# The last slice of a spectral convolution in halves, and its first output tile in two column parts

## The chip, the cores and the metric

The kernel runs on one core of one Trainium2 chip. The metric is device time in microseconds (us) of one execution. The core has five engines with instruction queues of their own: TensorE (PE in the profile, with PEld for its weight loads), VectorE (DVE), ScalarE (ACT), GpSimd (POOL) and SyncE (SP, which here only issues DMAs). Each engine takes its own instructions in order, and waits for others through semaphores.

## The reference

Four stages follow each other on a sequence x of 2048 tokens with 512 channels, each adding its result to x:

```
x = x + A(layernorm(x))     # long convolution, one filter per channel
x = x + B(layernorm(x))     # local dilated attention
x = x + A(layernorm(x))
x = x + B(layernorm(x))
```

A makes a filter K of 2048 lags for every channel from the state space parameters, multiplies the transforms of filter and input, transforms back, and adds u * Dskip:

```
y = irfft(rfft(u padded to 4096) * rfft(K padded to 4096))[:2048] + u * Dskip
```

B projects to q, k and v (32 heads of 16), lets every token attend to 8 tokens at distances 0, 2, ..., 14, and projects back. All data are bfloat16.

## The kernel before

The filters' spectra are computed once, at the start, and lie in DRAM (`kt_scratch`). Both A stages use them. `a_steps` builds one convolution. The transform has two stages: the first leaves Z, and then the 512 channels are taken in 16 slices of 32 channels, numbered cg from 0 to 15. A slice goes through a relay of steps, each named by a letter:

- T (L250): eight transposes of Z on TensorE into PSUM, `pt`; t (L256): the copy `zt` of it to SBUF, on VectorE mostly.
- X (L262): two matmuls of 512 columns, `xp`; c (L266): ScalarE copies them to `xc`, 128 x 1024, bfloat16.
- p (L270): VectorE multiplies `xc` with the spectrum `Kt` of the slice, which a DMA has brought (L232), into `pab`, 128 x 2048.
- v (L281): the inverse second stage, 16 pairs of a weight load (from `pab`) and a matmul of 128 columns, into `vp`, two PSUM banks for eight groups g.
- V (L285): ScalarE copies `vp`, reordered, to the slice's 32 of the 512 channels of VT.

In the first convolution the order of these steps stands at the end of the string KGEN, written out by hand (L336 to L354; it ends `@v13 @c15 @v14 @V13 @p15 @V14 @v15 @V15`). In the second it is the loop of `a_layer` (L299 to L310). `vp` and the tiles that follow share two PSUM buffers (tag psg in the first, psS in the second), so v of slice 15 needs the buffer that V of slice 13 frees, and the first y tile the one that V of slice 14 frees.

Then the inverse first stage: `y_rows(g, hf)` (L317) fills a PSUM tile `ps_y` of two times 128 rows x 512 channels, with three matmuls of 512 columns each: two against VT (L323, L324) and one with the identity that adds the old X (L327). The last group, g = 3, has a fourth (L326), which adds a correction `kU` for the last token. `kU` is computed by four VectorE instructions on one partition (L314 and three at L316), which are issued after the last instruction that `a.last` names: the product p of slice 15.

`b_layer` takes the eight tiles one by one. `y_group` (L1345) makes ScalarE copy each to X (L1361; with row sums at L1356 for two rows of group 1 in the first B stage), and `norm` follows for each group of four rows: statistics on VectorE (L1057, aggregated at L1060), logarithm and exponential on ScalarE (L1063, L1064), the bias (L1065) and the normalised rows N (L1073 on VectorE, L1071 on ScalarE). TensorE transposes N (L1087), ScalarE and VectorE copy it to `xnT` (L1090), and the q and k projections begin (L1104). The order of B's instructions comes from a planner (`Plan`) with estimated durations; the framework that builds the program then places instructions of neighbouring parts among each other.

Of the kernel before, what the change touches and what calls it, by code (L numbers as in the profile page):

```python
# [12 lines left out]
ALU = mybir.AluOpType  # L13
AX = mybir.AxisListType
F32 = mybir.dt.float32
BF = mybir.dt.bfloat16
# [4 lines left out]
D = 512  # L21
# [5 lines left out]
NG = 4  # L27
EPS = 1e-5
NM = 128
GE = 4  # L30
NGR = D // GE
# [185 lines left out]
def a_steps(nc, tc, C, Ng, kt_dram, load_w, layer, Z, es, es_y, psS=None):  # L217

    def pool(name, bufs=1, es=es, **kw):
        return es.enter_context(tc.tile_pool(name=name, bufs=bufs, reuse_waits="tile", **kw))  # L220
    fwork = pool("a_fwork", 2)
    a = SimpleNamespace(es_y=es_y)
    VT = a.VT = pool("a_vt", 1, es_y, side="right").tile([128, 2, NJ, D], BF, name="VT")
    pabp = pool("a_pab", 3 if layer == 0 else 4, es_y, side="right")
    F1T = a.F1T = pool("a_big", 1, es_y, side="right").tile([128, NJ, 2, 128], BF, name="F1Tsb")
    kts, pts, zts, xps, xcs, pabs, vps = {}, {}, {}, {}, {}, {}, {}

    def load_k(cg, eng=nc.sync):
        kts[cg] = fwork.tile([128, 8, 2, 128], BF, name="Kt", tag="Kt", bufs=KT_BUFS[layer])
        rows = kt_dram.ap()[:, cg * 32:(cg + 1) * 32].rearrange("k (e g) a l -> k e (g a l)", e=GE)  # L230
        for h in range(2):
            eng.dma_start(kts[cg][h::2].rearrange("q g a l -> q (g a l)"), rows)  # L232

    def load_f1t():
        nc.sync.dma_start(F1T[:], C["F1T_h"].ap())

    if layer == 0:
        with tc.issue_after(C["powers_used"].ins):
            load_f1t()
    for cg in range(6 if layer else 4):  # L240
        with tc.issue_after(C[FIRST_LOADS[cg]].ins) if layer == 0 else nullcontext():
            load_k(cg, nc.gpsimd if layer == 0 and FIRST_LOADS[cg][0] == "rows_end" else nc.sync)
    psT = pool("a_psT", 2, space=PSUM)
    psX = pool("a_psX", 1, space=PSUM)
    a.psS = psS or pool("a_psS", 2, es_y, space=PSUM, side="right")

    def transposes(cg):
        pt = pts[cg] = psT.tile([128, 8, 128], BF, name="pt", tag="psT")
        for g in range(8):
            nc.tensor.transpose(pt[:, g, :], Z[:, cg * 8 + g, :], C["ident"][:])  # L250
        if cg == 0 and layer:
            load_f1t()

    def transposed(cg, on_act=False):
        zts[cg] = fwork.tile([128, 8, 128], BF, name="zt", tag="zt", bufs=3)
        (nc.scalar.copy if on_act else nc.vector.tensor_copy)(zts[cg][:], pts.pop(cg)[:])  # L256

    def second_stage(cg):
        xps[cg] = psX.tile([128, 2, 512], F32, name="xp", tag="psX")
        zt = zts.pop(cg)[:].rearrange("q g k -> q (g k)")  # L260
        for h in range(2):
            nc.tensor.matmul(xps[cg][:, h, :], C["C2"][:], zt[:, h * 512:(h + 1) * 512], start=True, stop=True)  # L262

    def second_stage_out(cg):
        xcs[cg] = fwork.tile([128, 8, 1, 128], BF, name="xc", tag="xc")
        nc.scalar.copy(xcs[cg][:].rearrange("q g o l -> q (g o l)"), xps.pop(cg)[:].rearrange("q h n -> q (h n)"))  # L266

    def times_spectrum(cg):
        pabs[cg] = pabp.tile([128, 8, 2, 128], BF, name="pab", tag="pab")
        a.last = nc.vector.tensor_tensor(pabs[cg][:], xcs.pop(cg)[:].to_broadcast([128, 8, 2, 128]), kts.pop(cg)[:], ALU.mult)  # L270
        if layer and cg + KT_BUFS[layer] < 16:
            load_k(cg + KT_BUFS[layer])
        if cg == 14 and layer == 0:
            load_w()

    def inverse(cg):
        vp = vps[cg] = a.psS.tile([128, 8, 128], F32, name="vp", tag="psS" if psS is None else "psg")
        pab = pabs.pop(cg)
        for g in range(8):
            for ab in range(2):  # L280
                nc.tensor.matmul(vp[:, g, :], pab[:, g, ab, :], C["IC"][:, ab, :], start=(ab == 0), stop=(ab == 1))  # L281

    def inverse_out(cg):
        dst = VT[:].rearrange("k r j d -> k (r j) d")[:, :, cg * 32:(cg + 1) * 32]
        nc.scalar.copy(dst.rearrange("k q (e g) -> k q e g", e=GE), vps.pop(cg)[:].rearrange("k g (q e) -> k q e g", e=GE))  # L285

    a.step = dict(T=transposes, t=transposed, a=lambda cg: transposed(cg, True), X=second_stage, c=second_stage_out,
                  p=times_spectrum, v=inverse, V=inverse_out, k=load_k)
    return a


def a_layer(nc, tc, C, Xg, Ng, kt_dram, layer, Z, es_z, a=None):

    if a is None:
        with ExitStack() as es:
            es.enter_context(es_z)
            a = a_steps(nc, tc, C, Ng, kt_dram, None, layer, Z, es, ExitStack())
            with tc.manual_schedule():
                for cg in range(-2, 18):  # L299
                    if 0 <= cg < 16:  # L300
                        a.step["X"](cg)
                        a.step["c"](cg)
                    if cg + 2 < 16:
                        a.step["T"](cg + 2)
                        a.step["t"](cg + 2)
                    if cg >= 2:
                        a.step["v"](cg - 2)
                        a.step["V"](cg - 2)
                    if 0 <= cg < 16:
                        a.step["p"](cg)  # L310
    VT, F1T, psS, tag, ident = a.VT, a.F1T, a.psS, "psg" if layer == 0 else "psS", C["ident"]
    kU = Ng[NG - 1]
    with tc.issue_after(a.last.ins):
        nc.vector.tensor_tensor(kU[0:1], Ng[0][0:1], C["klast"][:].unsqueeze(1).to_broadcast([1, 4, D]), ALU.mult)  # L314
    for i in range(1, 4):
        nc.vector.tensor_tensor(kU[0:1, i, :], kU[0:1, i - 1, :], kU[0:1, i, :], ALU.add)  # L316
    def y_rows(g, hf):  # L317

        ps = psS.tile([128, 2, D], F32, name="ps_y", tag=tag)
        for jj in range(2):  # L320
            j4 = hf * 2 + jj
            j = g * 4 + j4
            nc.tensor.matmul(ps[:, jj, :], F1T[:, j, 0, :], VT[:, 0, j, :], start=True, stop=False)  # L323
            nc.tensor.matmul(ps[:, jj, :], F1T[:, j, 1, :], VT[:, 1, j, :], start=False, stop=False)  # L324
            if g == NG - 1:
                nc.tensor.matmul(ps[:, jj, :], C["last_tok"][:], kU[:, j4, :], start=False, stop=False)  # L326
            nc.tensor.matmul(ps[:, jj, :], ident[:], Xg[g][:, j4, :], start=False, stop=True)  # L327
        return ps
    return y_rows, a.es_y


# [1081 lines left out]
def kernel(  # L1413
# [71 lines left out]
    def open_conv(psS):  # L1485
        const2 = ctx.enter_context(tc.tile_pool(name="const2", bufs=1, side="right", reuse_waits="tile"))
        weights, load_w = load_b_weights(nc, const2, C, B_wqkv, B_wo)
        Wt.update(weights)
        return a_steps(nc, tc, C, Ng, kt_dram, load_w, 0, Z, es_z, es_y, psS)
# [37 lines left out]
```

## Time and profile before

| | us |
|---|---|
| three timed runs | 443.84, 444.71, 446.14 |
| their median | 444.71 |
| profiled execution, span from first to last instruction | 443.4 |
| profiled execution, own time | not listed |
| last VT copy of the first convolution, start to end | 154.14 to 155.15 |
| last VT copy of the second convolution, start to end | 320.60 to 321.61 |
| mean granted TensorE clock | 0.977 |

Times inside the kernel are counted from the first instruction of the profiled execution. In a timeline a line has the start, the duration (of all its instructions together where there are several), the engine, the line of the kernel, the operation with its output and inputs, the number of instructions, and in brackets how long the engine stood idle before it and what ended that. In a table by stage the columns are the stretch, its length, the busy time of PE, PEld, DVE, ACT and POOL with the number of instructions, the granted TensorE clock as a share of full speed, the DMA share and GB/s. In a line of groups, the numbers behind the first bar are the busy time in all and the mean of one in ns. Matmuls are pipelined: a matmul of 512 columns shows 0.38 us but the next starts 0.216 us after it.

### The profile page before, as it was taken

Reading aid. Unit: us, or ns where it says so; the run is one execution under the profiler, and the core shown is the slowest. Engines: PE = TensorE matmul, PEld = TensorE weight load, DVE = VectorE, ACT = ScalarE, POOL = GpSimd, SP = SyncE. Lnnn points to the kernel's source line nnn. Section 1 sums busy time; section 2 is a strip of 40 time slices with the busy share of each in tenths; the row PEclk is TensorE's granted clock in tenths of the full one; section 3 lists DMA queues with packets and bytes.
Section 4 is the critical chain, followed back from the end, with each engine's and each line's share of the span. In section 5 each row is a group of like instructions: output and inputs, shape, how many; then the busy total and the mean of one; then the engine's idle time right before and its main releaser. Section 6 shows DMA issues by size and latency. Waiting matters only on the chain.

```text
span 443.4 us, 12211 instructions
## 1 busy us (share of the span) xinstructions
PE 382.9 (86%) x5019; PEld 262.4 (59%) x5057; DVE 404.9 (91%) x816; ACT 332.8 (75%) x593; POOL 25.6 (6%) x66
## 2 busy tenths in 40 slices
PE   1176798999989799999998999689798999996896
PEld 1032585685478645687766554268645667885663
DVE  6999999998899968798999999899869899999994
ACT  6999988998899989657554499789968656762352
POOL 5000012013000000010020000000000000211000
PEclk9999799999999999999998999999989999998899
DMA  8900002254879900007061037169100000348022
GB/s 238 415 6 1 1 18 61 81 161 126 258 233 301 305 19 3 1 19 151 1 133 37 2 109 205 70 182 266 32 0 3 2 1 1 90 81 164 3 96 96
DMA packets 25646, 44.05 MB, mean 99 GB/s; under 512 B 7285, under 2 KB 17206, under 8 KB 24950
## 3 DMA queue, kind: packets, MB, share of 16 engines
q1 hardware_dynamic: 22630, 37.30, 29.4%
q0 software_dynamic: 1856, 4.53, 4.1%
q10 hardware_dynamic: 1104, 1.44, 0.9%
q8 instruction: 39, 0.64, 0.7%
q14 instruction: 17, 0.14, 0.1%
HBM read 29.01 MB, written 6.95 MB: 81 GB/s over the span
## 4 chain that ended last, share of the span: by engine, by line
PE 44%; DVE 25%; ACT 14%; issue 8%; DMA 6%; SPq 1%; DVEq 0%; POOLq 0%; ACTq 0%
DVE prodpv L1273 10%; PE ps_qk L1104 10%; DVE prodqk L1143 4%; PE psk L545 4%; PE Lp L1163 4%; PE ps_v L1178 3%; PE psg L578 3%; DMA Kt<-kt_scratch 3%; DVE Z L481 3%; PE ps_o L1310 2%; ACT xc L266 2%; ACT Z L1340 2%; PE pt L250 2%; PE po L1282 2%; DMA wo_t<-in_B_wo_dram 2%
## 5 line engine op out<-in xcount | busy, mean ns | idle before, releaser
L1143 DVE TENSOR_TENSOR prodqk<-qT,N 128x1024 bf16<-128x1024 bf16 (+3 forms) x176 | 83.7, 538 | 4.7 <-ACT qT L1106 2.7
L1273 DVE TENSOR_TENSOR prodpv<-V,Lsb 128x512 bf16<-128x512 bf16 (+2 forms) x144 | 80.0, 624 | 0.5 <-PE po L1282 0.4
L1104 PE MATMUL ps_qk<-xnT,wqk 128*128 128x512 bf16 x256 | 61.2, 379 | 1.1 <-ACT xnT L1090 1.1
L1282 PE MATMUL po<-halves,prodpv 128*128 128x64 bf16 x1024 | 44.8, 199 | 6.0 <-DVE prodpv L1273 4.5
L1282 PEld LDWEIGHTS <-prodpv 128*128 128x128 bf16 x1024 | 39.3, 102 | 16.2 <-DVE prodpv L1273 9.6
L270 DVE TENSOR_TENSOR pab<-xc,Kt 128x2048 bf16<-128x2048 bf16 x32 | 39.1, 1223 | 3.9 <-ACT xc L266 3.0
L1104 PEld LDWEIGHTS <-wqk 128*128 128x128 bf16 x256 | 23.4, 97 | 23.5 <-DVE xnT L1090 1.0
L266 ACT CAST xc<-xp 128x1024 bf16<-128x1024 f32 x32 | 34.1, 1066 | 4.1 <-PE xp L262 3.4
L1294 ACT CAST oT<-po 128x512 bf16<-128x512 f32 x32 | 17.6, 588 | 25.3 <-PE po L1282 25.3
L285 ACT CAST VT<-vp 128x1024 bf16<-128x1024 f32 x32 | 34.0, 1075 | 2.7 <-PE vp L281 2.7
L281 PE MATMUL vp<-sb_IC,pab 128*128 128x128 bf16 x512 | 33.5, 219 | 1.9 <-DVE pab L270 1.7
L281 PEld LDWEIGHTS <-pab 128*128 128x128 bf16 x512 | 30.4, 98 | 5.9 <-DVE pab L270 2.0
L1163 PEld LDWEIGHTS <-prodqk 128*128 128x128 bf16 x1024 | 30.8, 96 | 4.3
L1178 PE MATMUL ps_v<-wv,xnT 128*128 128x256 bf16 x256 | 31.7, 272 | 0.0
L1163 PE MATMUL Lp<-sb_bones,prodqk 128*128 128x8 bf16 x1024 | 30.9, 166 | 0.0
L1057 DVE BATCH_NORM_STATS2 ln_stats<-X 128x6 f32<-128x512 bf16 x37 | 23.7, 679 | 7.7 <-ACT X L1361 7.3
L1185 ACT CAST V<-ps_v 128x512 bf16<-128x512 f32 x32 | 18.7, 587 | 13.0 <-PE ps_v L1178 13.0
L1106 ACT CAST N<-ps_qk 128x512 bf16<-128x512 f32 x32 | 18.8, 588 | 11.6 <-PE ps_qk L1104 11.1
L505 PE MATMUL psadd<-Z,sb_ident 128*128 128x512 bf16 (+3 forms) x49 | 16.2, 345 | 12.8 <-DVE Z L481 8.2
L1310 PE MATMUL ps_o<-wo_t,oT 128*128 128x512 bf16 x96 | 26.3, 379 | 0.7 <-ACT oT L1294 0.3
L1178 PEld LDWEIGHTS <-xnT 128*128 128x128 bf16 x256 | 24.1, 98 | 3.8
L1106 ACT CAST qT<-ps_qk 128x512 bf16<-128x512 f32 x32 | 18.6, 585 | 8.7 <-PE ps_qk L1104 8.6
(199 smaller groups left out, 815.0 us busy)
## 6 DMA issues: line engine op xcount, KB each, us to landing
Kt<-kt_scratch SPq DMA_DIRECT2D x60, 256.0 KB
kt_scratch<-ks SPq DMA_DIRECT2D x32, 128.0 KB
G<-c_G SPq DMA_DIRECT2D x2, 1536.0 KB
V<-V SPq DMA_DIRECT2D x8, 288.0 KB
X<-in_A_u_dram SPq DMA_DIRECT2D x4, 512.0 KB
F1Tsb<-c_F1T SPq DMA_DIRECT2D x2, 1024.0 KB
V<-V SPq DMA_DIRECT2D x4, 512.0 KB
V<-V POOLq DMA_DIRECT2D x4, 384.0 KB, 6.5
```

The costliest lines, as they stand in the source:

```text
L266: nc.scalar.copy(xcs[cg][:].rearrange("q g o l -> q (g o l)"), xps.pop(cg)[:].rearrange("q h n -> q (h n)"))
L270: a.last = nc.vector.tensor_tensor(pabs[cg][:], xcs.pop(cg)[:].to_broadcast([128, 8, 2, 128]), kts.pop(cg)[:], ALU.mult)
L281: nc.tensor.matmul(vp[:, g, :], pab[:, g, ab, :], C["IC"][:, ab, :], start=(ab == 0), stop=(ab == 1))
L285: nc.scalar.copy(dst.rearrange("k q (e g) -> k q e g", e=GE), vps.pop(cg)[:].rearrange("k g (q e) -> k q e g", e=GE))
L1104: nc.tensor.matmul(t.ps[:], wqk[:, ct, f0:f0 + 128], x_group(g)[:, :, ct], start=(ct == 0), stop=(ct == 3))
L1106: return plan.add("ACT", act_us(512), lambda: nc.scalar.copy(dst[:, g * 512:(g + 1) * 512], t.ps[:]), [p] + list(free), drop=[p])
L1143: nc.vector.tensor_tensor(b.pr[:, u:u + 2 * n, 1 - halves_of[0], :], q, cols(kT[i][:, starts[0]:starts[0] + n * 128]), ALU.mult)
L1163: nc.tensor.matmul(t.Lp[:, w, u % 2, u // 2, :], b.pr[:, u].rearrange("f a q -> f (a q)"), bones[:], start=False, stop=(t.parts == W // 2 ...
L1178: nc.tensor.matmul(t.ps[:, jj, :], tokens(ct, jp * 2 + jj, c), wv[:, ct, fp * 256:(fp + 1) * 256], start=(jj + ct == 0), stop=(jj == 1 and ...
L1273: nc.vector.tensor_tensor(t.p2[:, c:c + k, 0:nj, :].rearrange("p c j (d h) -> p c j d h", d=DH), m.V2[i // 2][:, c0 + c:c0 + c + k, r0:r0 ...
L1282: nc.tensor.matmul(po[jj // k][:, jj % k, c, :], t.p2[:, c - c0, jj, :], fold, start=(c == 0 and w == 0 and jj % k == 0), stop=(c == 1 and ...
L1310: nc.tensor.matmul(t["ps"][:], m.oT[:, ft, j * 128:(j + 1) * 128], wo_t[:, ft, :], start=(added and ft == 0), stop=False)
```

## The change

For slice 15 alone (`parts` gives the groups 0 to 3 and 4 to 7 for it, and all eight in one for the others) the copy of `xp` to `xc`, the product with the spectrum, and the copy of `vp` to VT are each made in two instructions, by groups. The second half of the VT copy is on VectorE, and `a.last`, after which the kU work is issued, is now that copy. The first y tile of each convolution is computed in two column parts: the channels 0 to 479, which slices 0 to 14 fill, and the channels 480 to 511 of slice 15. So it has six matmuls of 480 columns and six of 32, in place of six of 512.

```diff
@@ -225,6 +225,10 @@
     F1T = a.F1T = pool("a_big", 1, es_y, side="right").tile([128, NJ, 2, 128], BF, name="F1Tsb")
     kts, pts, zts, xps, xcs, pabs, vps = {}, {}, {}, {}, {}, {}, {}
 
+    def parts(cg):
+
+        return (slice(0, 4), slice(4, 8)) if cg == NGR // 8 - 1 else (slice(0, 8),)
+
     def load_k(cg, eng=nc.sync):
         kts[cg] = fwork.tile([128, 8, 2, 128], BF, name="Kt", tag="Kt", bufs=KT_BUFS[layer])
         rows = kt_dram.ap()[:, cg * 32:(cg + 1) * 32].rearrange("k (e g) a l -> k e (g a l)", e=GE)
@@ -262,12 +266,17 @@
             nc.tensor.matmul(xps[cg][:, h, :], C["C2"][:], zt[:, h * 512:(h + 1) * 512], start=True, stop=True)
 
     def second_stage_out(cg):
-        xcs[cg] = fwork.tile([128, 8, 1, 128], BF, name="xc", tag="xc")
-        nc.scalar.copy(xcs[cg][:].rearrange("q g o l -> q (g o l)"), xps.pop(cg)[:].rearrange("q h n -> q (h n)"))
+        xc, xp = fwork.tile([128, 8, 1, 128], BF, name="xc", tag="xc"), xps.pop(cg)
+        xcs[cg] = xc
+        for gs in parts(cg):
+            nc.scalar.copy(xc[:, gs].rearrange("q g o l -> q (g o l)"), xp[:].rearrange("q h n -> q (h n)")[:, gs.start * 128:gs.stop * 128])
 
     def times_spectrum(cg):
-        pabs[cg] = pabp.tile([128, 8, 2, 128], BF, name="pab", tag="pab")
-        a.last = nc.vector.tensor_tensor(pabs[cg][:], xcs.pop(cg)[:].to_broadcast([128, 8, 2, 128]), kts.pop(cg)[:], ALU.mult)
+        pab, xc, kt = pabp.tile([128, 8, 2, 128], BF, name="pab", tag="pab"), xcs.pop(cg), kts.pop(cg)
+        pabs[cg] = pab
+        for gs in parts(cg):
+            n = gs.stop - gs.start
+            nc.vector.tensor_tensor(pab[:, gs], xc[:, gs].to_broadcast([128, n, 2, 128]), kt[:, gs], ALU.mult)
         if layer and cg + KT_BUFS[layer] < 16:
             load_k(cg + KT_BUFS[layer])
         if cg == 14 and layer == 0:
@@ -281,8 +290,13 @@
                 nc.tensor.matmul(vp[:, g, :], pab[:, g, ab, :], C["IC"][:, ab, :], start=(ab == 0), stop=(ab == 1))
 
     def inverse_out(cg):
-        dst = VT[:].rearrange("k r j d -> k (r j) d")[:, :, cg * 32:(cg + 1) * 32]
-        nc.scalar.copy(dst.rearrange("k q (e g) -> k q e g", e=GE), vps.pop(cg)[:].rearrange("k g (q e) -> k q e g", e=GE))
+        dst = VT[:].rearrange("k r j d -> k (r j) d")[:, :, cg * 32:(cg + 1) * 32].rearrange("k q (e g) -> k q e g", e=GE)
+        src = vps.pop(cg)[:].rearrange("k g (q e) -> k q e g", e=GE)
+        for gs in parts(cg):
+            if gs.start:
+                a.last = nc.vector.tensor_copy(dst[..., gs], src[..., gs])
+            else:
+                nc.scalar.copy(dst[..., gs], src[..., gs])
 
     a.step = dict(T=transposes, t=transposed, a=lambda cg: transposed(cg, True), X=second_stage, c=second_stage_out,
                   p=times_spectrum, v=inverse, V=inverse_out, k=load_k)
@@ -317,14 +331,16 @@
     def y_rows(g, hf):
 
         ps = psS.tile([128, 2, D], F32, name="ps_y", tag=tag)
-        for jj in range(2):
-            j4 = hf * 2 + jj
-            j = g * 4 + j4
-            nc.tensor.matmul(ps[:, jj, :], F1T[:, j, 0, :], VT[:, 0, j, :], start=True, stop=False)
-            nc.tensor.matmul(ps[:, jj, :], F1T[:, j, 1, :], VT[:, 1, j, :], start=False, stop=False)
-            if g == NG - 1:
-                nc.tensor.matmul(ps[:, jj, :], C["last_tok"][:], kU[:, j4, :], start=False, stop=False)
-            nc.tensor.matmul(ps[:, jj, :], ident[:], Xg[g][:, j4, :], start=False, stop=True)
+        for cols in (slice(0, D - 32), slice(D - 32, D)) if g + hf == 0 else (slice(0, D),):
+            for jj in range(2):
+                j4 = hf * 2 + jj
+                j = g * 4 + j4
+                end = cols.stop == D
+                nc.tensor.matmul(ps[:, jj, cols], F1T[:, j, 0, :], VT[:, 0, j, cols], start=(cols.start == 0), stop=False)
+                nc.tensor.matmul(ps[:, jj, cols], F1T[:, j, 1, :], VT[:, 1, j, cols], start=False, stop=False)
+                if g == NG - 1:
+                    nc.tensor.matmul(ps[:, jj, cols], C["last_tok"][:], kU[:, j4, cols], start=False, stop=False)
+                nc.tensor.matmul(ps[:, jj, cols], ident[:], Xg[g][:, j4, cols], start=False, stop=end)
         return ps
     return y_rows, a.es_y
```

## Prediction

> **What bounds the kernel now.** I read the head of the page and its chain first. No engine bounds all of it: VectorE is busiest, TensorE carries most of the chain.
>
> ```profile
> span 443.4 us, 12211 instructions
> PE 382.9 (86%) x5019; PEld 262.4 (59%) x5057; DVE 404.9 (91%) x816; ACT 332.8 (75%) x593; POOL 25.6 (6%) x66
> PE 44%; DVE 25%; ACT 14%; issue 8%; DMA 6%; SPq 1%; DVEq 0%; POOLq 0%; ACTq 0%
> ```
>
> So a change is worth what it does to its own stage. It touches two stages, the ends of the two convolutions. The timeline of the second, from its last product to the first copy of y:
>
> ```profile
> 318.04 1.97 ACT L285 CAST VT<-vp 128x1024 bf16<-128x1024 f32 x2
> 318.21 1.23 DVE L270 TENSOR_TENSOR pab<-xc,Kt 128x2048 bf16<-128x2048 bf16 x1 [0.61 <-ACT xc L266]
> 319.49 1.07 PE L281 MATMUL vp<-sb_IC,pab 128*128 128x128 bf16 x16 [0.72 <-DVE pab L270]
> 320.60 1.01 ACT L285 CAST VT<-vp 128x1024 bf16<-128x1024 f32 x1 [0.59 <-PE vp L281]
> 321.66 0.38 PE L323 MATMUL ps_y<-VT,F1Tsb 128*128 128x512 bf16 x1 [1.10 <-ACT VT L285]
> 324.08 1.01 ACT L1361 CAST X<-ps_y 128x1024 bf16<-128x1024 f32 x1 [2.47 <-PE ps_y L327]
> ```
>
> It is a relay: one engine works on slice 15 while the others wait. xc (ACT, 317.14), pab (DVE), vp (PE), VT (ACT), first y row (PE). The same relay in the first convolution:
>
> ```profile
> 151.75 1.23 DVE L270 TENSOR_TENSOR pab<-xc,Kt 128x2048 bf16<-128x2048 bf16 x1 [0.81 <-DMA Kt<-kt_scratch]
> 153.04 1.07 PE L281 MATMUL vp<-sb_IC,pab 128*128 128x128 bf16 x16 [0.97 <-DVE pab L270]
> 154.14 1.01 ACT L285 CAST VT<-vp 128x1024 bf16<-128x1024 f32 x1 [0.89 <-PE vp L281]
> 155.20 0.38 PE L323 MATMUL ps_y<-VT,F1Tsb 128*128 128x512 bf16 x1 [1.10 <-ACT VT L285]
> ```
>
> Here the last slice also waited for its Kt, until 151.75. The last view is the table by stage around the second end, with the granted clock in the eighth column ("us" is the first):
>
> ```profile
> 318.61:322.02 3.41, 1.59 (x20) 1.14 (x19) 3.18 (x5) 2.42 (x3) 0.00 (x0) 1.00 0.02 5
> 322.02:325.43 3.41, 3.32 (x9) 1.22 (x8) 0.30 (x1) 1.01 (x1) 0.00 (x0) 0.50 0.00 0
> 325.43:328.84 3.41, 3.41 (x17) 1.57 (x16) 2.64 (x9) 2.14 (x3) 0.00 (x0) 1.00 0.00 0
> ```
>
> After the waits, TensorE ran 3.41 us at 0.50; that cost half of it, 1.7 us, since y keeps TensorE full. In the first convolution the stretch 151.35 to 154.76, with 1.79 us of TensorE work against 1.59, was followed by full clock.
>
> **What the change does to each relay.** In the built order of instructions the changed tail is: xc in two, pab in two, eight vp pairs, then *one y matmul of 480 columns, which waits for VT of slice 14*, then the other eight vp pairs, five y matmuls of 480 columns, six of 32. ScalarE's half of the last VT copy waits for all sixteen pairs, and VectorE's half waits for ScalarE's half. So the two halves of the copy run one after the other, and half of the vp pairs stand behind VT of slice 14. The prices:
>
> ```profile
> L1143 DVE TENSOR_TENSOR prodqk<-qT,N 128x1024 bf16<-128x1024 bf16 x80 | 52.6, 684 | 4.7 <-ACT qT L1106 2.7 <-ACT N L1106 1.7 <-PE Lp L1163 0.3
> L1340 DVE CAST Z<-ps_s 128x512 bf16<-128x512 f32 x10 | 6.5, 684 | 0.5 <-PE ps_s L1337 0.4
> L1294 ACT CAST oT<-po 128x512 bf16<-128x512 f32 x32 | 17.6, 588 | 25.3 <-PE po L1282 25.3
> ```
>
> - A half product costs 0.68 us (1.23 whole). It is no longer on the path: TensorE waits later for VT of slice 14 and for its buffer.
> - xc in two: 1024-wide copies start 0.91 us apart (150.26 to 151.17), 512-wide ones 0.50 apart (eleven at L1340 in 5.51 us). So 2 x 0.50 - 0.91 = 0.09 us more on ScalarE, ahead of VT of slices 13 and 14, and now on the path.
> - Half a VT copy on ScalarE: 0.59 us; on VectorE, reading float32 from PSUM and scattering runs of four, 0.69 (the nearest row, L1340, also scatters by fours). In a row 1.28 instead of 1.01, plus one hand-over of 0.03. The half copy itself isn't in the trace: at best 0.43 (half of the 0.686 row at L256 and a start-up of 0.09), at worst 1.01, the whole copy.
> - vp: sixteen pairs issue in 0.89, so 0.056 each; eight take 0.45, and 0.17 until the last one's result is out.
> - A 480-wide y matmul: 0.20 (0.216 x 480/512). The 32-wide ones: between the 128x8 rows (L1163, 48 in 1.18 us, 0.025 each) and the 128-wide (0.056), so six cost 0.15 to 0.33; I take 0.15, since 32 is nearer 8.
> - In all 12 more matmuls with their weight loads, two more copies on ScalarE, four more instructions on VectorE; no DMA is added, and SP's and POOL's queues keep their order.
>
> *First convolution.* VT of slice 14 ends at 151.17 + 2.08 + 0.09 = 153.34; y480 starts at 153.39; the rest of vp 153.59 to 154.21; VT halves 154.24 to 154.83 and 154.86 to 155.55; six narrow matmuls from 155.59; the second y tile starts at 155.74. Before: 155.20 + 6 x 0.216 = 156.50. That is 0.76 earlier. The five other 480s (1.0 us) lie under the two copies.
>
> VectorE must not spoil it. Its half copy is followed by the kU work (L314, L316: 1.24 + 3 x 0.43 = 2.53 us), which before ran at 152.90, during the relay, and now starts at 155.5, partly between the statistics of the first y rows: 155.5 + 2.53 + 4 x 0.64 + 0.35 = 160.9, against 160.60 before. There it had 1.02 us of idle time next (161.62), waiting for a ScalarE copy that now comes 0.7 earlier. So 0.1 is lost and the first transposes of N (163.48) come **0.65 us** earlier. From 163.5 to 184 TensorE has almost no gap, so this passes on.
>
> *Second convolution.* VT of slice 14 ends at 320.10, y480 320.15, vp to 320.97, VT halves to 321.60 and 322.32, second y tile at 322.51. At full clock the old one would be at 321.66 + 1.30 = 322.96: 0.45 gained on TensorE, and 2.1 against the profiled execution if the slow stretch goes too (0.45 + 1.7). But VectorE has no reserve here. All four rows of the first group are its own, so from 322.25 it has 2.53 + 4 x 0.64 + 0.33 and ends its aggregates at 327.7. The profile shows them ending at 328.74 with the slow clock, which is 327.04 without it. From 328.66 to 341.94 VectorE has almost no gap, and its last product there, N of the third group (340.59 to 341.94), is what TensorE takes at 341.95. So VectorE's time decides: **-1.05 us against the profiled execution, +0.65 against one with full clock**.
>
> **A rule about the clock.** The half-speed stretches in this trace begin at 48.95, 236.69, 322.02, 400.42 and 410.66: apart by 55, 25, 23 and 3 times 3.413 us. They stand on a grid. Nothing in the rows ties the grid to the kernel's start, so I take its phase as chance from one execution to the next. With the relay's idle time as it was, a 3.41 us stretch with under about 1.7 us of TensorE work fits at some 0.8 of 3.41 us of phases (window starts), so one tail in four is slow. In the new tail the longest idle pieces are 0.5 to 0.6 us and the work in any such stretch is 2 us or more.
>
> [...]
>
> **The sum.** Against the profiled execution: -0.65 - 1.05 = -1.7, a span of 441.7. What lies around the span isn't listed: the three timed runs are 443.84 to 446.14, 0.4 to 2.7 above it, so I apply differences to their median, 444.71. In a typical execution the second end is somewhere between -1.05 and +0.65; near the middle, and nearer to the full clock, I take -0.05. Forecast: 444.71 - 0.65 - 0.05 = **444.0**. One part in 200 (2.2 us) is about what a measurement of this kernel can tell from no change.
>
> **Rivals.**
> 1. *The clock is the gain.* If slow stretches at the tails are common in the timed runs, both go: -0.65 - 1.05 and up to 1.2 more for the first tail, 441.8 to 443.0. For: the stretch at 322. Against: one of two tails here.
> 2. *VectorE becomes the bound and the clock drops later* (slower). kU work moved behind the copy makes the second tail 0.65 late; TensorE then waits some 2.2 us (333.1 to 335.35) between its transposes and the first q/k projection, where the profile has 1.3. A 3.41 us stretch around that holds 1.2 us of work, less than the 1.59 that was followed by half clock, so about two in five executions would lose up to 1.7 after it. It decides once the kU work ends after the first X copy, 323.7; I have it at 324.8. Time: 444.71 - 0.65 + 0.65 + 1.5 = 446.2.
> 3. *The halves don't overlap enough.* If VectorE's half copy costs 1.0 (0.31 more) and the narrow matmuls 0.33 (0.18 more), the first tail gains 0.15 instead of 0.65, and VectorE is 0.65 + 0.31 late in the second: 444.71 - 0.15 + 0.96 = 445.5. For: the halves wait for each other. Against: L1340's 0.684 for the same shape.
>
> **Chances.** Forecast (443.0 to 444.9) 0.52; rival 1 0.20; rival 2 0.16; rival 3 0.12. The range, 442.2 to 446.0, leaves out the ends of rivals 1 and 2. Of rival 1 and its neighbours 0.12 lies below 442.5 (faster by over 0.5%); of rival 2, where both tails lose, 0.09 lies above 446.9; the rest, 0.79, is within.
>
> **What will show it.** Right: ScalarE's half VT copy at 0.59 and VectorE's right behind it at 0.69; the first 480-wide matmul right behind VT of slice 14; the second y tile 0.7 us after the end of the first convolution's last VT copy, not 1.35; no 0.50 clock within 4 us of either tail; kU work between the statistics. Wrong: vp's second half not behind y480, VectorE idle after 323 in the second tail, or a slow stretch at the first q/k projection. The forecast fails if the later stages, each with its own clock stretches, move by more than the tails.

## The result and the profile after

| | before | after |
|---|---|---|
| median, us (runs) | 444.85 (20) | 442.84 (20) |
| lowest to highest | 442.94 to 446.66 | 441.82 to 444.03 |
| ratio after/before, 95% interval | | 0.9953 [0.9941, 0.9966] |
| profiled execution: span, own time | 443.4, not listed | 441.7, 443.47 |

The change made the kernel 2.0 us faster (0.47%). The forecast was 0.7 (444.0). 442.84 lies outside the forecast's own band (443.0 to 444.9) and in that of rival 1; only the range, which is wide (442.2 to 446.0), holds it. The loss that the forecast put against the gain did not come.

The head of the page and the chain of waits of the kernel after. There are 50 more matmul records and VectorE is as busy as before; TensorE now carries 53% of the chain in place of 44%, but this is not a size of the effect: a second trace of the same kernel (`c_after`) has 50%, and `e_ku`, which has the same relays, 45%.

```profile
span 441.7 us, 12278 instructions
PE 385.9 (87%) x5069; PEld 262.8 (60%) x5069; DVE 405.3 (92%) x820; ACT 332.1 (75%) x595; POOL 25.3 (6%) x66
PE 53%; DVE 21%; ACT 16%; issue 7%; DMA 2%; DVEq 0%; SPq 0%; ACTq 0%
```

(12 of the 50 are the change's own. Before's trace has 5019 matmuls to 5057 weight loads, after's 5069 to 5069, so the other 38 are records that were missing. xc is now L272, pab L279, vp L290, VT L299 on ScalarE and L297 on VectorE, y L339 to L343.) The end of the second convolution in the timeline of the kernel after:

```profile
318.25 1.29 DVE L279 TENSOR_TENSOR pab<-xc,Kt 128x1024 bf16<-128x1024 bf16 x2 [0.18 <-ACT xc L272]
...
320.60 0.36 PE L339 MATMUL ps_y<-VT,F1Tsb 128*128 128x480 bf16 x1 [0.31 <-ACT VT L299]
320.80 0.61 PE L290 MATMUL vp<-sb_IC,pab 128*128 128x128 bf16 x8
321.44 0.58 ACT L299 CAST VT<-vp 128x512 bf16<-128x512 f32 x1 [0.90 <-PE vp L290]
322.06 0.69 DVE L297 CAST VT<-vp 128x512 bf16<-128x512 f32 x1 [2.51 <-ACT VT L299]
...
322.80 0.18 PE L339 MATMUL ps_y<-VT,F1Tsb 128*128 128x32 bf16 x1 [0.39 <-DVE VT L297]
...
322.95 0.38 PE L339 MATMUL ps_y<-VT,F1Tsb 128*128 128x512 bf16 x1
```

Read it from the brackets. The 480-wide matmul waits for VT of slice 14, and the last eight pairs stand behind it; the pairs' products have been ready since 319.54 (318.25 + 1.29). Then the two half copies run one behind the other, 0.58 and 0.69 us. The last line is the second y tile. Relative to the start of the copy xc of slice 15 (317.60 here, 317.14 before) it begins after 5.35 us; before, at full clock, after 321.66 + 6 x 0.216 - 317.14 = 5.82. So this relay is 0.47 us shorter. The end of the first convolution, same view:

```profile
154.62 0.36 PE L339 MATMUL ps_y<-VT,F1Tsb 128*128 128x480 bf16 x1 [0.31 <-ACT VT L299]
...
155.47 0.58 ACT L299 CAST VT<-vp 128x512 bf16<-128x512 f32 x1 [0.90 <-PE vp L290]
156.08 0.69 DVE L297 CAST VT<-vp 128x512 bf16<-128x512 f32 x1 [2.02 <-ACT VT L299]
...
156.98 0.38 PE L339 MATMUL ps_y<-VT,F1Tsb 128*128 128x512 bf16 x1
```

xc began at 151.52, so 5.46 us; before 156.50 - 150.26 = 6.24. That is 0.78 shorter, of which up to 0.30 is before's wait for Kt (to 151.75), which no longer stands on the path. Together the two relays lost **1.25 us**. The table by stage around the second end has no half-speed stretch (granted clock in the eighth column):

```profile
318.30:321.70 3.40, 2.65 (x37) 2.10 (x35) 1.25 (x2) 2.50 (x4) 0.00 (x0) 1.00 0.02 5
321.70:325.10 3.40, 3.01 (x20) 1.36 (x19) 3.00 (x5) 1.99 (x3) 0.00 (x0) 1.00 0.00 0
```

TensorE has 2.65 us of work in a stretch where before had 1.59.

### The profile page after: what moved, and what is told of

The parts are those of the page before. It is cut to its first block, busy times and chain, and to the rows that moved or that the text cites. A ratio compares the mean times of both kernels' runs of the same rounds, so it can differ in the third digit from the quotient of the medians.

```text
span 441.7 us, 12278 instructions
## 1 busy us (share of the span) xinstructions
PE 385.9 (87%) x5069; PEld 262.8 (60%) x5069; DVE 405.3 (92%) x820; ACT 332.1 (75%) x595; POOL 25.3 (6%) x66
## 3 DMA queue, kind: packets, MB, share of 16 engines
q10 hardware_dynamic: 1104, 1.44, 0.9%
## 4 chain that ended last, share of the span: by engine, by line
PE 53%; DVE 21%; ACT 16%; issue 7%; DMA 2%; DVEq 0%; SPq 0%; ACTq 0%
PE ps_qk L1120 10%; DVE prodpv L1289 7%; PE psk L561 6%; PE ps_o L1326 4%; PE Lp L1179 4%; DVE prodqk L1159 4%; PE ps_v L1194 3%; PE po L1298 3%; ACT xc L272 3%; PE psg L594 3%; DVE Z L497 2%; PE xp L266 2%; ACT Z L1356 2%; PE vp L290 2%; PE pt L254 2%
## 5 line engine op out<-in xcount | busy, mean ns | idle before, releaser
L279 DVE TENSOR_TENSOR pab<-xc,Kt 128x2048 bf16<-128x2048 bf16 (+1 forms) x34 | 39.2, 1160 | 3.3 <-ACT xc L272 3.2
L272 ACT CAST xc<-xp 128x1024 bf16<-128x1024 f32 (+1 forms) x34 | 34.3, 1020 | 4.1 <-PE xp L266 4.1
L299 ACT CAST VT<-vp 128x1024 bf16<-128x1024 f32 (+1 forms) x32 | 33.2, 1052 | 3.1 <-PE vp L290 2.7
L290 PE MATMUL vp<-sb_IC,pab 128*128 128x128 bf16 x512 | 33.8, 219 | 0.9 <-ACT VT L299 0.9
L290 PEld LDWEIGHTS <-pab 128*128 128x128 bf16 x512 | 30.6, 98 | 6.0 <-issue 1.4
L521 PE MATMUL psadd<-Z,sb_ident 128*128 128x512 bf16 (+3 forms) x50 | 17.7, 368 | 12.8 <-DVE Z L497 8.6
```

The costliest lines, as they stand in the source:

```text
L272: nc.scalar.copy(xc[:, gs].rearrange("q g o l -> q (g o l)"), xp[:].rearrange("q h n -> q (h n)")[:, gs.start * 128:gs.stop * 128])
L279: nc.vector.tensor_tensor(pab[:, gs], xc[:, gs].to_broadcast([128, n, 2, 128]), kt[:, gs], ALU.mult)
L299: nc.scalar.copy(dst[..., gs], src[..., gs])
```

## The experiments

Three accounts were to be told apart. **A**: the shorter relays pass on whole (some 1.2 us), and the rest of the gain, 0.5 to 0.8, is half-speed stretches that no longer follow the waits at the two ends. **B**: the clock plays no part. **C**, the prediction's: VectorE, late because the kU work comes behind its half copy, decides the second convolution. In two of the kernels only parts of the change are there, and two others keep TensorE busy without shortening a relay.

Column parts alone (`e_cols`: before, with only this edit):

```diff
-        for jj in range(2):
+        for cols in (slice(0, D - 32), slice(D - 32, D)) if g + hf == 0 else (slice(0, D),):
+            for jj in range(2):
...
```

> The kernel before with only the first y tile in column parts (480, 32); the last slice is whole and ScalarE makes its whole VT copy. If the two halves of the VT copy in a row and the pairs of the inverse stage behind the 480-wide matmul cost what the after trace shows, this is the better half: the six 480-wide matmuls lie under the VT copy, and the second y tile starts 0.2 us after its end (1.15 us earlier than before in each convolution). Theory A: 2.3 us of relay and 0.8 of clock, 441.7. If instead the halves carry the gain: no more than 0.4 us faster than before.

Halves alone (`e_halves`: after, with `y_rows` of before):

```diff
-        for cols in (slice(0, D - 32), slice(D - 32, D)) if g + hf == 0 else (slice(0, D),):
-            for jj in range(2):
+        for jj in range(2):
...
```

> The changed kernel with the first y tile whole again: only the last slice in halves, the second half of its VT copy on VectorE. Theory A: the relay is 0.3 us shorter in the first convolution and no shorter in the second, and TensorE is idle nearly as long as before, so 444.4 to 444.8. If the halves carry the gain: 443.0 to 443.5.

The kernel after once more, beside them (`c_after`):

> The changed kernel again, as the control beside the others. Both theories: some 2.0 us faster than before, as in the result (442.8 against 444.85).

Fillers (`e_fill`: before, with matmuls that nobody reads in the waits of the relay):

```diff
+        if cg == 15:
+            nc.tensor.matmul(vp[:, 0:4, :].rearrange("k g n -> k (g n)"), C["ident"][:], C["zero"][:].to_broadcast([128, 512]), start=True, stop=True)
...
+        if g + hf == 0:
+            for _ in range(5):
+                nc.tensor.matmul(ps[:, 0, :], ident[:], C["zero"][:].to_broadcast([128, 512]), start=True, stop=True)
```

> The kernel before with filler matmuls (512 columns of zeros against the identity, into the PSUM tile that the next real matmuls overwrite): one ahead of the last slice's sixteen pairs, five ahead of the first y tile, in each convolution. The relay stays as long as before; only TensorE's idle time in it is filled. Theory A (the gain of 2.0 us is 1.1 to 1.2 of shorter relays and some 0.8 of half-speed stretches that no longer follow them): 0.8 us faster than before, 444.0, and no clock of 0.50 within 4 us of either tail. Theory B (the clock plays no part, all 2.0 us are the shorter relays): no difference, 444.8 to 445.

Measured beside the same before (444.59 us, 24 runs): `e_cols` 441.84, ratio 0.9938 [0.9916, 0.9961]; `e_halves` 443.98, 1.0003 [0.9979, 1.0027]; `c_after` 443.03, 0.9963 [0.9948, 0.9978]; `e_fill` 447.45, 1.0063 [1.0038, 1.0087]. The ratio is not the quotient of the two medians; the two differ most where a kernel's runs scatter (`e_halves`: 442.57 to 447.03).

The column parts alone gain more than the whole change: five of the six runs of `e_cols` are at 442.14 or below, and of the 32 of the kernel after only four. The halves alone gain nothing that can be told from zero. The end of the second convolution in the timeline of `e_cols`:

```profile
318.48 1.07 PE L281 MATMUL vp<-sb_IC,pab 128*128 128x128 bf16 x16 [0.72 <-DVE pab L270]
319.38 0.37 PE L325 MATMUL ps_y<-VT,F1Tsb 128*128 128x480 bf16 x1
319.58 1.01 ACT L285 CAST VT<-vp 128x1024 bf16<-128x1024 f32 x1 [0.59 <-PE vp L281]
...
320.80 0.38 PE L325 MATMUL ps_y<-VT,F1Tsb 128*128 128x512 bf16 x1
```

The sixteen pairs run in one go, ahead of the 480-wide matmuls, and these then lie under the one whole copy. The second y tile starts 4.68 us after xc (316.12), against 5.35 in the kernel after. And of `e_halves`:

```profile
319.36 0.58 ACT L299 CAST VT<-vp 128x512 bf16<-128x512 f32 x1 [0.23 <-PE vp L290]
319.98 0.69 DVE L297 CAST VT<-vp 128x512 bf16<-128x512 f32 x1 [1.84 <-ACT VT L299]
320.72 0.38 PE L337 MATMUL ps_y<-VT,F1Tsb 128*128 128x512 bf16 x1 [1.40 <-DVE VT L297]
```

Here the pairs start earlier, which wins 0.3, and the two half copies give it back: 319.36 to 320.67 is 1.31 us against 1.01 for the whole one. The relay is 5.82 us, as before.

`e_fill` does not answer its question:

```profile
321.59 1.25 PE L324 MATMUL ps_y<-zero_col,sb_ident 128*128 128x512 bf16 x5 [0.54 <-ACT VT L287]
322.67 1.05 PE L283 MATMUL vp<-sb_IC,pab 128*128 128x128 bf16 x16
```

The framework put the five fillers of y ahead of the last sixteen pairs. They need the PSUM buffer that VT of slice 14 frees, so the pairs, whose product was there at 320.97 (319.74 + 1.23), waited until 322.67. The relays became 1.32 and 1.65 us longer, which is the loss. The 480-wide matmul ahead of the second eight pairs does the same thing in the kernel after, on a smaller scale. So the fillers were held behind the last pair (`e_fill2`), and the same was done to the 480-wide matmul of the kernel after (`e_order`). Of two more kernels, `e_ku` undoes one part of the change, and `e_mix` puts the better parts together.

`e_fill2` (on before) and `e_order` (on after), where `a.last_v` is the matmul of the last pair:

```diff
+            with tc.issue_after(a.last_v.ins):
+                for _ in range(5):
+                    nc.tensor.matmul(ps[:, 0, :], ident[:], C["zero"][:].to_broadcast([128, 512]), start=True, stop=True)
```

```diff
+                with tc.issue_after(a.last_v.ins) if g + hf + jj + cols.start == 0 else nullcontext():
                     nc.tensor.matmul(ps[:, jj, cols], F1T[:, j, 0, :], VT[:, 0, j, cols], start=(cols.start == 0), stop=False)
```

> The kernel before with five filler matmuls (512 columns of zeros against the identity, into the first y tile's buffer before its real matmuls overwrite it), this time ordered behind all sixteen pairs of the last slice, in each convolution. They fill 1.08 of the 1.28 us in which TensorE waits for the last VT copy, and the relay must keep its length (second y tile 1.30 us after the end of that copy, all at full clock). Theory A (a part of the gain is that half-speed stretches no longer follow the tails): 0.4 to 0.8 us faster than before. Theory B (all of the gain is shorter relays): no difference.

> The changed kernel with one ordering more: the first 480-wide y matmul is issued behind all sixteen pairs of the last slice. By the traces the eight pairs that stood behind it came out 0.7 us late in each convolution. Theory A (relay time passes on whole): 1.3 us faster than the changed kernel, 441.5 to 441.7. Rival (VectorE, which still makes half a VT copy and then the correction for the last token, sets the pace after the second convolution): at most 0.7 faster, 442.2 or more.

`e_ku` (after, with the kU work behind the product again):

```diff
-            nc.vector.tensor_tensor(pab[:, gs], ...
+            a.last = nc.vector.tensor_tensor(pab[:, gs], ...
...
-                a.last = nc.vector.tensor_copy(dst[..., gs], src[..., gs])
+                nc.vector.tensor_copy(dst[..., gs], src[..., gs])
```

> The changed kernel with the correction for the last token (four VectorE instructions, 2.5 us) issued behind the last product again, as before, and not behind the half VT copy. The step of the prediction that VectorE's lateness decides in the second convolution: 0.6 to 0.9 us faster than the changed kernel. Theory A (VectorE has reserve enough, as the after trace says): within 0.3 us of the changed kernel, or slower by the delay if the half copy has to wait for one of the four.

`e_mix` (both edits of `e_order` and `e_ku`, and the last VT copy whole on ScalarE; xc and pab stay in halves):

```diff
-        for gs in parts(cg):
-            if gs.start:
-                a.last = nc.vector.tensor_copy(dst[..., gs], src[..., gs])
-            else:
-                nc.scalar.copy(dst[..., gs], src[..., gs])
+        nc.scalar.copy(dst, src)
```

> xc and the product of the last slice in halves, its VT copy whole on ScalarE, the first y tile in column parts behind all sixteen pairs. Theory A: the relay is 0.3 us shorter in the second convolution and 0.6 in the first than with the column parts alone (441.84), because the inverse pairs begin earlier: 440.8 to 441.2. Rival (the buffer that the copy of slice 13 frees and the later start of the copies take it back): no faster than the column parts alone.

Measured beside one before (444.96 us, 24 runs): `e_fill2` 443.65, 0.9976 [0.9949, 1.0003]; `e_order` 441.93, 0.9938 [0.9915, 0.9961]; `e_ku` 443.44, 0.9974 [0.9956, 0.9992]; `e_mix` 441.33, 0.9924 [0.9900, 0.9948]. Timeline of `e_order`:

```profile
318.49 1.05 PE L290 MATMUL vp<-sb_IC,pab 128*128 128x128 bf16 x16 [0.43 <-ACT VT L299]
...
321.10 0.38 PE L340 MATMUL ps_y<-VT,F1Tsb 128*128 128x512 bf16 x1
```

With the sixteen pairs in one go again, the second y tile starts 4.68 us after xc (316.42), as in `e_cols`. Its time, 441.93, lies between what its two theories gave (441.5 to 441.7, and 442.2 or more), nearer the first. `e_ku` is not faster than the kernel after, where C gave 0.6 to 0.9. `e_fill2` decides nothing: its interval takes in both of its theories. And of `e_mix`:

```profile
318.69 1.05 PE L290 MATMUL vp<-sb_IC,pab 128*128 128x128 bf16 x16 [0.43 <-ACT VT L295]
319.60 0.36 PE L336 MATMUL ps_y<-VT,F1Tsb 128*128 128x480 bf16 x1
319.78 1.01 ACT L295 CAST VT<-vp 128x1024 bf16<-128x1024 f32 x1 [0.23 <-PE vp L290]
...
320.99 0.38 PE L336 MATMUL ps_y<-VT,F1Tsb 128*128 128x512 bf16 x1
```

The half products let the pairs start earlier (2.08 us after xc, 316.61, against 2.36 in `e_cols`), nothing comes between the pairs, and one copy follows. All six runs of `e_mix` (440.87 to 441.62) are below the lowest of the 32 of the kernel after (441.82). Against `e_cols` (441.31 to 442.85) its median is 0.5 us lower, where 0.9 was expected; the relays differ by 0.3 in each convolution, not by 0.3 and 0.6, and the runs of the two overlap, so what the half products add isn't shown by the times.

**All kernels by their relays.** For each, the time from the start of xc of slice 15 to the second y tile, in the first and the second convolution, less that of before (6.24, 5.82), next to the measured difference (ratio less 1, times before's median) and the granted clock, a mean over its runs:

| | relays, us | their sum | measured, us | clock |
|---|---|---|---|---|
| before (48 runs) | | | | 0.970 |
| after | -0.78, -0.47 | -1.25 | -2.1 [-2.6, -1.5] | 0.976 |
| c_after | -0.78, -0.47 | -1.25 | -1.6 [-2.3, -1.0] | 0.978 |
| e_ku | -0.78, -0.47 | -1.25 | -1.2 [-2.0, -0.4] | 0.976 |
| e_cols | -1.45, -1.14 | -2.59 | -2.8 [-3.7, -1.7] | 0.974 |
| e_order | -1.45, -1.14 | -2.59 | -2.8 [-3.8, -1.7] | 0.978 |
| e_mix | -1.75, -1.44 | -3.19 | -3.4 [-4.4, -2.3] | 0.973 |
| e_halves | -0.31, 0 | -0.31 | +0.1 [-0.9, +1.2] | 0.972 |
| e_fill | +1.32, +1.65 | +2.97 | +2.8 [+1.7, +3.9] | 0.974 |
| e_fill2 | -0.22, 0 | -0.22 | -1.1 [-2.2, +0.1] | 0.975 |

The relays lie within the interval of every row but the first. They are most of the measured size in `e_cols`, `e_order`, `e_mix`, `e_fill` and `c_after`, all of it in `e_ku`, and 1.25 of 2.1 in after; in `e_halves` and `e_fill2` the intervals take in zero. One term of the column is not firm. Before's first relay, 6.24, holds a wait for Kt: the product starts 1.49 us after xc. In `e_cols`, `e_fill` and `e_fill2`, which build the last slice in the same way, it starts 1.18 to 1.27 us after xc, and the bracket names xc, not Kt. If that wait is chance of the one execution, up to 0.3 us has to be added to each sum (after and `c_after` -0.95, the latter then at the edge of its interval; `e_cols` -2.29, `e_fill` +3.27, `e_halves` 0).

Account C falls. In each of the ten traces the first q/k projection starts 11.43 to 11.44 us after the second y tile in the first convolution, and 12.09 to 12.11 in the second (before's with its slow stretch taken off: 336.75 - 1.70 - 322.96). It makes no difference whether VectorE's aggregates end 4.1 us after that tile (kU work ahead of them) or 4.6 to 4.7 (kU work among them). So a shorter relay passes on whole to the q/k projection. `e_ku` shows it directly. There one kU product and one addition run ahead of the half copy, and the other two additions (0.85 us) behind it:

```profile
324.81 0.36 DVE L1076 BATCH_NORM_AGGREGATE ln_mv<-ln_stats 128x2 f32<-128x6 f32 x4
...
333.18 1.02 PE L1120 MATMUL ps_qk<-xnT,wqk 128*128 128x512 bf16 x4 [1.12 <-ACT xnT L1106]
```

Its aggregates end 9.45 us after xc (315.72) against 10.05 in the kernel after (327.65 - 317.60), and the projection starts 17.46 after xc in both. VectorE 0.60 us earlier gains nothing, which C can't have.

Between A and B the runs decide less sharply. For A: the mean granted clock rises from 0.970 (48 runs, standard error 0.001) to 0.976 (32 runs, 0.001) with the change. In the traces, one of the four ends with the old waits (two in before, two in `e_halves`) is followed by a half-speed stretch, and none of the twelve ends of the six traces with column parts. The kernels that were to separate the causes are too noisy for it: 0.972 where the halves alone leave TensorE's waits in place, 0.975 where fillers alone take them away, and 0.973 for `e_mix`, each with a standard error of 0.002. Over the runs of one kernel the time falls by about 0.8 us for 0.01 more clock (0.77 in before, 0.85 in after, standard errors 0.2 and 0.3), so 0.006 goes with some 0.5 us, an estimate. By another way it comes out larger: one stretch of 3.41 us at 0.50 takes 0.0039 from the mean of 443 us, so 0.006 is 1.5 stretches fewer per execution, and at the 1.7 us of before's second end that would be 2.6 us, more than there is to explain. Against a large share: the relays leave 0.2 for `e_cols`, `e_order` and `e_mix`, nothing for `e_ku`, 0.8 for after and `e_fill2` (up to 0.3 more each by the wait for Kt), and `e_fill2`'s interval takes in zero. I take the clock's part as 0 to 0.8 us, most likely near 0.5. That it has a part is argued, not shown.

## Why the forecast was too small

- *First relay, -0.76: right.* -0.78 measured, by the same trace of before, with its wait for Kt. Its terms held: halves 0.58 and 0.69, half copies in a row with 0.04 between, narrow matmuls 0.025 apart (322.80 to 322.95 for six). The 0.1 that VectorE was to lose didn't come: the transposes of N start 12.44 us after xc (163.96 - 151.52) against 13.22 (163.48 - 150.26), the whole 0.78.
- *Second relay, -0.45 on TensorE: right.* -0.47 measured.
- *"So VectorE's time decides": the step that failed.* It made -0.45 into +0.65 at full clock. VectorE's lines after the end in the kernel after, and the first q/k projection, there and (last line) in before:

```profile
327.30 0.35 DVE L1076 BATCH_NORM_AGGREGATE ln_mv<-ln_stats 128x2 f32<-128x6 f32 x4
...
334.28 0.66 DVE L1106 COPY xnT<-pt_x 128x1024 bf16<-128x1024 bf16 x1
...
335.06 1.02 PE L1120 MATMUL ps_qk<-xnT,wqk 128*128 128x512 bf16 x4 [1.12 <-ACT xnT L1106]
...
336.75 1.02 PE L1104 MATMUL ps_qk<-xnT,wqk 128*128 128x512 bf16 x4 [1.12 <-ACT xnT L1090]
```

  The aggregates end at 327.65. xc stands 0.46 later here than before, so in before's time that is 327.19; I had 327.7. I had priced the kU additions at 0.43 each, from a run in which each uses the last one's result, and the statistics at 0.64, from two in 1.29, which counts the last one's end. Here they take turns (323.91, 324.25, 324.85, 325.18): an addition is followed after 0.33, a statistic after 0.60. And the stretch behind them, which I took as full, had room. From the end of the aggregates to the end of N of the third group VectorE took 13.20 us in before (328.74 to 341.94), busy for 12.87 of them, and 12.60 here (327.65 to 340.25), without a gap. These 0.5 and 0.6 are the 1.1 us between +0.65 and -0.45. Nor is it VectorE that the projection waits for: in both kernels the bracket names ScalarE's copy to xnT, 1.12 us. The projection starts at 335.06, or 334.60 in before's time; before had it at 336.75 with its slow stretch, 335.05 without. So 0.45 arrives: the whole of TensorE's gain.
- *The clock: mis-sized, as far as the runs tell.* The forecast's -0.05 at the second end gives a slow stretch a weight of 0.41 (0.70 of the 1.70 us between its two cases), against VectorE's +0.65, and the first end gets nothing. Without the VectorE step, and with the stretches as rare as I had them (one tail in four, 1.7 us each, so some 0.4 a tail), the same sum gives -0.78 - 0.47 - 0.8 = -2.05 us. Measured were -2.1 and -1.6. That it fits may be luck: the 0.8 is at the upper end of what the runs leave to the clock. The limit behind it, under some 1.7 us of work in a stretch, was an estimate from two rows (1.59 us of work before 0.50, 1.79 before 1.00) and isn't firm: in before's trace the stretch from 233.28 to 236.69 holds 2.21 us of matmuls and is followed by 0.50 too. That the phase of the stretches is chance, which the weight rests on too, was an assumption from one trace; the phases of the three traces in the last section differ.
- *Rivals.* Rival 1 named the right time, 441.8 to 443.0, but its larger part is the relays, not the clock. Rival 2 did not come: TensorE waits 1.12 us ahead of the first q/k projection, as before, not 2.2, and the clock stays at 1.00 there. Rival 3 fell with 0.69 and 0.025.
- *What I saw and didn't use.* The working noted that the second eight pairs stand behind VT of slice 14 and that the half copies add 0.28, but not that the column parts alone would do better. `e_cols` and `e_order` put 1.3 us on it by their relays.

## What to carry to other kernels

Follow a relay by its links, and make a change to each link separately: of two edits that go together one can carry the whole gain (here 2.6 us of relay for the column parts alone, none clear of noise for the halves alone), and the order in which their instructions are built can take half of it back (1.3 us, by `e_order`). Splitting a copy between two engines is no gain where the second half waits for the first (1.31 us against 1.01 here); filling the copy's time with matmuls that don't need it is (the relays of `e_cols` are 1.45 and 1.14 us shorter). Before an engine without idle time is called the bound of a moved step, add up what the moved instructions cost where they now stand, interleaved (0.33 us for an addition and 0.60 for a statistic here, against 0.43 and 0.64), look for the small waits behind them, and see which engine the next stage waits for.

## What the hardware showed that I had not expected

- In these traces the half-speed stretches stand on a grid that isn't tied to the program. In before's execution two begin at 236.69 and 322.02, 25.0 times 3.413 us apart; in after's, two at 49.80 and 401.38, 103.0 times that apart. But from before's 322.02 to after's 401.38 it is 23.25 times, so the phase differs. It differs with the same kernel too: in the other trace of the kernel after (`c_after`) the clock is 0.50 from 50.70, 0.26 of a stretch behind after's 49.80.
- The profiled execution of after had the lower mean clock, 0.969 against 0.977, and was yet 1.7 us shorter. Before's has six half-speed stretches of 3.41 us, one of them at the second end; after's has eight, three of them in a row from 49.8 to 60.0, and none at the ends. The relays (1.25) and the stretch at the second end (1.7) would make it 2.95 us shorter, so the three more stretches elsewhere cost some 1.2 us in all, an estimate. Here the mean clock said little of what a stretch costs.
- The spread of the times differs from kernel to kernel: before runs from 442.5 to 446.7, `e_order` from 441.64 to 442.23 (7 runs), `e_mix` from 440.87 to 441.62 (6 runs). It isn't TensorE's waits alone that set it: with the waits filled, `e_fill2` runs from 441.32 to 447.44 (12 runs). The cause stays open.
- The time of an execution is 1.7 to 1.9 us above its span in each run that has both on record (443.47 and 441.7 for the profiled one of the kernel after), where the three timed runs of before had let me guess 0.4 to 2.7.
